# Mask buffers cut to the size in use in an attention and FFN kernel, and where the buffers behind them begin

## The chip, the cores and the metric

The kernel runs on one core of one Trainium2 chip. The metric is the device time of one execution in microseconds. In the profile, PE is TensorE's matmul, PEld its weight load, DVE is VectorE, ACT is ScalarE, POOL is GpSimd, and SP is the engine whose queue issues nearly all DMAs.

## The reference

A banded (sliding window) attention is followed by a feed-forward network (FFN) with two weight matrices. The batch is 8, with 8 heads, 576 tokens and a head dimension of 64, so the FFN sees 4608 tokens of 512 values; its inner width is 2048. Everything is float32.

```
scores = scale * np.matmul(q, k.transpose(0, 1, 3, 2))
mask = (rel >= 0) & (rel < window)          # rel = query - key position, window = 64
scores = np.where(mask, scores, -1000000000.0)
attn = softmax(scores)
x = (attn @ v) as [4608 tokens, 512]
h = x @ w_in                                # 512 -> 2048
g = np.where(h >= 1, h, np.where(h <= -1, 0.0, (h + 1) ** 2 / 4))
out = g @ w_out                             # 2048 -> 512
```

## The kernel before

The tokens are cut into nine FFN tiles of 512, and each of them into four attention steps of 128 tokens. An attention step loads qt, kt and two vt tiles, makes the scores on PE (L418), adds a mask and scales on DVE (L435), takes the row maximum (L439), the exponentials on ACT (L446) and the division (L458), transposes the probabilities into ptd (L464 on DVE; L479 on PE for the first steps) and multiplies them with vt (L493). The result is one block of x.

The FFN works in float32r, a float32 type that TensorE takes in one pass, with each number split into a high and a low part: x into xh and xl, each weight into the two halves of a wts buffer, each gate into gh and gl. A product is made as high times high, high times low and low times high, so each matmul appears three times. In a matmul, lhsT is the stationary operand (loaded by PEld) and rhs the moving one (streamed by PE).

- L898 (`ffn_in`), for the first three tiles: stationary is a wts block of 128 columns, moving is xh or xl, 512 columns (256 where a tile is done in halves).
- L831 (`ffn_product`), for the other six tiles, which go in three pairs: each pair's first layer is computed from seven products of sums of blocks in place of eight. Stationary is a piece of the ring, which is loaded from DRAM into freed weights buffers; moving is one of six x operands, split into high and low. Two of the six lie in xs buffers (which share the memory of xh1 and xl1), the other four in freed wts buffers. In the profile's names these are `ps_h<-xs,wts` and `ps_h<-wts`.
- L950 (`ffn_out`), the second layer, for all tiles: stationary is a block of 128 columns of gh or gl, moving is a wts half of 512 columns.
- Between the layers, the gate runs through ACT (L911, L916, L928), DVE (L923) and POOL or DVE (L933). For the pairs, first-layer sums stand in h buffers (L846, in the memory of xh0 and xl0), and some are spilled to DRAM and loaded back.

The order on every engine is fixed when the program is built: a planner (`Plan`) places each step by a key and a cost table of constants, and nothing in it reads a buffer's address. Two masks concern the change. `nmsk` holds three mask variants for the steps that use 32-row queries and 96 keys; it is declared with three rows of 128 columns, of which 96 are loaded (L400) and read (L433). `mskr` is a rounded copy of `msk` for the first four steps, whose mask is added by a matmul (L412); it is declared with three variants, of which two are written (L404). `nm` and `den` (L424) hold the negated maxima and the sums, 2 x 4 numbers a step, two buffers each.

On-chip buffers are laid out in each partition in this order, one behind the other: constants (idt, msk, nmsk, idr, mskr, ptd), the x pool (xh0/h, xl0/h, xh1/xs, xl1/xs), loads (kt, qt, vt), attention (sm, nm, den), FFN (u, a, gh, gl, o), weights. Start addresses of the program before, in bytes:

| buffer | begins at | past a multiple of 256 | past a multiple of 512 |
|---|---|---|---|
| idt (first constant) | 2176 | 128 | 128 |
| nmsk | 4224 | 128 | 128 |
| ptd | 7808 | 128 | 128 |
| xh0 / h | 13952 | 128 | 128 |
| kt | 46720 | 128 | 128 |
| sm | 65152 | 128 | 128 |
| nm | 73344 | 128 | 128 |
| u | 73472 | 0 | 256 |
| a (first gate buffer) | 81664 | 0 | 256 |
| first weights buffer | 98048 | 0 | 256 |

All other buffers of a kind follow at multiples of 512 or, for kt (3072 bytes) and the like, of 1024.

Of the kernel before, what the change touches and what calls it, by code (L numbers as in the profile page):

```python
# [10 lines left out]
F32 = mybir.dt.float32  # L11
F32R = mybir.dt.float32r
# [8 lines left out]
P = 128  # L21
QB = 64
SB = 2 * QB
WIN = 128
WINDOW = 64
SQ = 32
NEAR = WINDOW + SQ
# [174 lines left out]
def banded_attention_then_ffn(ctx: ExitStack, tc: tile.TileContext, q, k, v, w, masks, out, dims):  # L202
    nc = tc.nc
    B, H, S, D = dims
    NT, DM = out.shape
    NP = H // 2
# [3 lines left out]
    scale = 1.0 / float(D) ** 0.5  # L210
    TMAX = max(TILES)

    const = ctx.enter_context(tc.tile_pool(name="const", bufs=1))
    xpool = ctx.enter_context(tc.tile_pool(name="xpool", bufs=1))
    ld = ctx.enter_context(tc.tile_pool(name="ld", bufs=2))
    att = ctx.enter_context(tc.tile_pool(name="att", bufs=4))
# [9 lines left out]
    def banks_of_heads(pool):  # L226
        return bank(pool).rearrange("p (a n) -> p a n", a=NP)
# [1 line left out]
    idt = const.tile([P, P], F32, name="idt")  # L229
    make_identity(nc, idt)  # L230
    msk = const.tile([P, 3, WIN], F32, name="msk")
    nmsk = const.tile([P, 3, WIN], F32, name="nmsk")
    idr = const.tile([P, P], F32R, name="idr")
    mskr = const.tile([P, 3, WIN], F32R, name="mskr")
    wpool = ctx.enter_context(tc.tile_pool(name="wpool", bufs=1))
    dram = ctx.enter_context(tc.tile_pool(name="dram", bufs=1, space=bass.MemoryType.DRAM))
    kept = [dram.tile([P, 7, 2, 2, P], F32, name=f"kept{n}") for n in range(NF // 2)]
# [3 lines left out]
    for n, at in ((P, QB), (QB, 0)):  # L241
# [4 lines left out]
            out=m, in_=m, compare_op=ALU.is_ge, fill=NEG, base=at - 1, pattern=[[1, WIN]], channel_multiplier=-1  # L246
        )
        nc.gpsimd.affine_select(
            out=m, in_=m, compare_op=ALU.is_ge, fill=NEG, base=WINDOW - at, pattern=[[-1, WIN]], channel_multiplier=1
# [129 lines left out]
    def variant(s):  # L379
        firsts = [(2 * s + i) % NB == 0 for i in range(2)]  # L380
        return 1 if firsts[0] else 2 if firsts[1] else 0

    def near(s):
        return s >= PE_STEPS
# [12 lines left out]
        nc.sync.dma_start(out=t, in_=v[b * QB:b * QB + WIN])  # L397

    def load_masks():
        nc.sync.dma_start(out=nmsk[:, :, :NEAR], in_=masks)  # L400

    def round_masks():
        nc.scalar.copy(idr, idt)
        nc.scalar.mul(mskr[:, :2], msk[:, :2], 1.0 / scale)  # L404

    def att_scores(s, masked, pool):
        qt, kt = qts.pop(s), kts.pop(s)
        banks = [banks_of_heads(pool) for _ in range(2)]
        if masked:
            m = mskr[:, variant(s), :].unsqueeze(1).broadcast_to([P, NP, WIN])  # L410
            for ps in banks:
                nc.tensor.matmul(ps.rearrange("p a n -> p (a n)"), lhsT=idr, rhs=m, start=True, stop=False)  # L412
        m, n = (SQ, NEAR) if near(s) else (QB, WIN)
        for p in range(NP):
            for i in range(SB // m):
                r = slice(i * m, (i + 1) * m)
                for h in range(2):
                    nc.tensor.matmul(  # L418
                        banks[h][r, p, :n], lhsT=qt[half[h], p, r], rhs=kt[half[h], p, i * m:i * m + n],
                        start=not masked, stop=not masked or p == NP - 1,  # L420
                    )
        sm = att.tile([P, 2 * NP * WIN], F32, name="sm", bufs=BUFS["sm"])[:, :2 * NP * n]
        sm = sm.rearrange("p (h a n) -> p h a n", h=2, n=n)
        nm, den = (att.tile([P, 2, NP], F32, name=n, bufs=2) for n in ("nm", "den"))  # L424
        for h in range(2):
            blk[s, h] = banks[h][:, :, :n], sm[:, h], nm[:, h], den[:, h]
        blk[s, BOTH] = None, sm, nm, den
# [171 lines left out]
    def add_step(t, i):  # L599
# [15 lines left out]
        if s == 0:  # L615
            last["r"] = add(lk, dict(ACT=480), lambda e: round_masks())
        if s == PE_STEPS - 2:
            last["m"] = add(lk + M_LATE, dict(SP=590), lambda e: load_masks(), lag=DMA_LAG)
# [6 lines left out]
        if before:  # L625
            sv, (needs_v, gives_v, split) = before.popitem()

            def do(e):
                att_scores(s, masked, ps)
                att_values(sv, "ps_h")  # L630

            xs = add(
                key, dict(PE=B_PE), do, needs + needs_v, takes=[ps, ps, "sm", "ps_h"],
                gives=[("qt", xq), ("kt", xk)] + gives_v,
            )
            split(xs, key, "ps_h")
        else:
            xs = add(
                key, dict(PE=S_PE[near(s)] + 500 * masked), lambda e: att_scores(s, masked, ps), needs,
                takes=[ps, ps, "sm"], gives=[("qt", xq), ("kt", xk)],  # L640
            )
# [599 lines left out]
```

## Time and profile before

| what | us |
|---|---|
| median of three runs | 888.4 (886.26 to 888.56) |
| profiled execution | 887.9 |
| its span, first to last instruction | 886.0 |
| PE busy in the span | 866.9 |
| DVE busy | 646.3 |
| ACT busy | 499.4 |
| POOL busy | 190.9 |

The span is the time from the first to the last instruction of the profiled execution; 1.9 us of that execution lie around it. PE's busy time adds up pipelined matmuls whose ends are modelled, so the duration of one matmul in a row (some 390 ns) is longer than the time until the next one starts. Where a text speaks of the step of a matmul, it means the time from one start to the next. In the chain's rows, the columns are start, length and what ran, both in us. In the timeline's rows they are start, length up to the end of the last matmul, and the group. In a row of groups, the two numbers behind the first bar are busy us and mean ns of one instruction, and behind the second bar stands the idle time before them.

### The profile page before, as it was taken

The numbers are of one execution on the slowest core, as the hardware profiler recorded it, in microseconds if no ns is written. First come the engines' busy times: TensorE is split into PE (matmuls) and PEld (weight loads), VectorE is DVE, ScalarE is ACT, GpSimd is POOL, SyncE is SP. The second block draws the span as 40 slices with busy tenths as digits, with TensorE's granted clock in tenths as the row PEclk, the third lists the DMA queues.
The fourth block names the chain that finished last, engine by engine and source line by source line (L and its number), as shares of the span: only waits on it lengthen the run. The fifth ranks groups of instructions, "written<-read, shape, count | busy, mean of one in ns | idle before, by whom it ended". The sixth has DMA issues, their size and how long they took to land.

```text
span 886.0 us, 17772 instructions
## 1 busy us (share of the span) xinstructions
PE 866.9 (98%) x6687; PEld 699.8 (79%) x6687; DVE 646.3 (73%) x1278; ACT 499.4 (56%) x1246; POOL 190.9 (22%) x202
## 2 busy tenths in 40 slices
PE   7899999999999999999999999999999999999998
PEld 5778887877777788877878788887887888888786
DVE  6999997888877776797888985587889633333443
ACT  6999965556464656545346864443548643333464
POOL 1000045554422352121113331111130011111000
PEclk8999999999999999999999999999999999999999
DMA  9992179445333313667666606676544045554221
GB/s 320 419 361 86 40 214 322 126 150 180 130 126 126 108 55 119 231 204 226 188 198 191 205 13 202 187 215 203 176 137 155 24 140 170 160 158 147 100 100 48
DMA packets 88372, 147.57 MB, mean 167 GB/s; under 512 B 7776, under 2 KB 36704, under 8 KB 88288
## 3 DMA queue, kind: packets, MB, share of 16 engines
q1 hardware_dynamic: 88000, 145.53, 50.9%
q8 instruction: 53, 0.87, 0.4%
q10 hardware_dynamic: 288, 0.92, 0.3%
q14 instruction: 31, 0.25, 0.1%
HBM read 112.86 MB, written 33.55 MB: 165 GB/s over the span
## 4 chain that ended last, share of the span: by engine, by line
PE 86%; DVE 6%; DMA 5%; ACT 2%; POOL 1%; issue 1%; ACTq 0%; DVEq 0%; POOLq 0%
PE acc L950 40%; PE ps_h L831 26%; PE ps_h L898 12%; PE ps_a L493 3%; PE ps_a L418 3%; DMA raw<-in_w 3%; DVE ptd L464 1%; DVE sm L458 1%; DMA kept<-u 1%; DVE a L923 1%; DMA out<-o 1%; ACT sm L446 1%; DMA kept<-o 1%; DVE gl L933 0%; DVE h L846 0%
## 5 line engine op out<-in xcount | busy, mean ns | idle before, releaser
L950 PE MATMUL acc<-wts,gh 128*128 128x512 f32 x1154 | 362.2, 395 | 2.1 <-ACT h L274 2.0
L950 PEld LDWEIGHTS acc<-wts,gh 128*128 128x128 f32 x1154 | 212.9, 188 | 51.5 <-ACT h L274 3.3
L950 PE MATMUL acc<-wts,gl 128*128 128x512 f32 x577 | 225.8, 391 | 1.4 <-DVE gl L933 0.8
L933 POOL TENSOR_TENSOR gl<-a,gh 128x512 fp32r<-128x512 f32 (+1 forms) x82 | 105.2, 1283 | 440.9 <-ACT gh L928 430.5
L831 PE MATMUL ps_h<-wts 128*128 128x512 f32 x720 | 179.1, 390 | 0.0
L831 PEld LDWEIGHTS ps_h<-wts 128*128 128x128 f32 x720 | 134.7, 188 | 28.7
L464 DVE STREAM_TRANSPOSE ptd<-sm 32x256 f32<-32x256 f32 x336 | 146.5, 436 | 6.3 <-PE ps_a L493 0.3
L846 DVE TENSOR_TENSOR h<-h,ps_h 128x512 f32<-128x512 f32 x120 | 82.2, 685 | 80.1 <-PE ps_h L831 79.0
L928 ACT CAST gh<-a 128x512 fp32r<-128x512 f32 (+1 forms) x149 | 89.5, 602 | 87.5 <-DVE a L923 79.4
L898 PE MATMUL ps_h<-xh,wts 128*128 128x512 f32 (+1 forms) x424 | 133.6, 382 | 4.6 <-DVE a L923 3.3
L950 PEld LDWEIGHTS acc<-wts,gl 128*128 128x128 f32 x577 | 108.4, 188 | 27.2 <-DVE gl L933 2.4
L911 ACT ACTIVATE a<-h 128x512 f32<-128x512 f32 x96 | 60.3, 631 | 101.2 <-DVE h L846 74.1
L923 DVE SCALAR_TENSOR_TENSOR a<-a,h 128x512 f32<-128x512 f32 x96 | 67.1, 700 | 65.5 <-ACT a L916 63.7
L446 ACT ACTIVATE sm<-sm,nm 128x96 f32<-128x96 f32 (+1 forms) x256 | 93.2, 366 | 19.0 <-DVE nm L439 19.0
L898 PEld LDWEIGHTS ps_h<-xh,wts 128*128 128x128 f32 x424 | 78.5, 191 | 21.5 <-DVE a L923 4.3
L916 ACT ACTIVATE a<-a 128x512 f32<-128x512 f32 (+1 forms) x136 | 83.8, 616 | 4.2
L898 PE MATMUL ps_h<-xl,wts 128*128 128x512 f32 (+1 forms) x212 | 80.0, 377 | 0.5 <-DVE xl L506 0.5
L831 PE MATMUL ps_h<-xs,wts 128*128 128x512 f32 x288 | 75.0, 395 | 0.0
L274 ACT COPY h<-ps_h 128x512 f32<-128x512 f32 x46 | 27.0, 587 | 74.4 <-PE ps_h L831 74.1
L831 PEld LDWEIGHTS ps_h<-xs,wts 128*128 128x128 f32 x288 | 53.7, 188 | 12.1
L911 ACT ACTIVATE a<-ps_h 128x512 f32<-128x512 f32 (+1 forms) x53 | 29.4, 554 | 42.1 <-PE ps_h L898 39.5
L933 DVE TENSOR_TENSOR gl<-a,gh 128x512 fp32r<-128x512 f32 (+1 forms) x67 | 44.7, 668 | 7.7 <-ACT gh L928 7.3
(106 smaller groups left out, 837.7 us busy)
## 6 DMA issues: line engine op xcount, KB each, us to landing
wts<-kept SPq DMA_DIRECT2D x168, 256.0 KB, 3.0
vt<-in_v SPq DMA_DIRECT2D x72, 256.0 KB, 3.6
kt<-in_k SPq DMA_DIRECT2D x35, 384.0 KB, 4.3
raw<-in_w SPq DMA_DIRECT2D x12, 1023.8 KB, 11.3
qt<-in_q SPq DMA_DIRECT2D x36, 256.0 KB, 3.1
spill<-h SPq DMA_DIRECT2D x18, 512.0 KB, 3.0
h<-spill SPq DMA_DIRECT2D x18, 512.0 KB, 3.7
out<-o SPq DMA_DIRECT2D x27, 256.0 KB, 2.5
```

Of the source, the lines that this page charges most:

```text
L274: nc.scalar.copy(dst, src)
L446: nc.scalar.activation(sm[:, p, :], (ps if masked else sm)[:, p, :], AF.Exp, bias=nm[:, p:p + 1], scale=scale if masked else 1.0, accum_ou ...
L464: nc.vector.transpose(dst[:, :, r], src[:, :, c * SQ:(c + 1) * SQ])
L831: nc.tensor.matmul(ps, lhsT=r[:, part, cp], rhs=x_op(k, xp)[:, cp], start=j in (0, 1, 3, 4) and i == 0 and cp == 0, stop=j in (1, 2, 5, 6) ...
L846: nc.vector.tensor_tensor(out=h[:, to], in0=h[:, of], in1=prods[u, n, b], op=ALU.add)
L898: nc.tensor.matmul(ps, lhsT=wts[f, 0][:, part, c * P:(c + 1) * P], rhs=x[:, c, r], start=(c == 0 and j == 0), stop=(c == NP - 1 and j == 2),)
L911: nc.scalar.activation(gs[t, f, r.start][0], phs[t, f, r.start], AF.Relu, bias=0.5, scale=0.5)
L916: nc.scalar.activation(a, a, AF.Square)
L923: nc.vector.scalar_tensor_tensor(out=a, in0=a, scalar=1.0, in1=ps, op0=ALU.min, op1=ALU.max)
L928: nc.scalar.copy(g[1], g[0])
L933: engine[eng].tensor_tensor(out=g[2], in0=g[0], in1=g[1].bitcast(F32), op=ALU.subtract)
L950: nc.tensor.matmul(acc[t, i][:, n], lhsT=g[:, sub], rhs=wts[f, 1][:, part, n], start=(q == 0 and j == 0), stop=(q == NF - 1 and j == 2 and ...
```

## The change

Three declarations shrink or grow, and three uses are adapted to them. `nmsk` gets rows of 96 columns in place of 128, so the transfer that fills it writes one contiguous run in a partition. `mskr` gets two variants in place of three. `nm` and `den` are taken from buffers of twice the size, of which the first half is used. No instruction is added or removed.

```
-    nmsk = const.tile([P, 3, WIN], F32, name="nmsk")
+    nmsk = const.tile([P, 3, NEAR], F32, name="nmsk")
     idr = const.tile([P, P], F32R, name="idr")
-    mskr = const.tile([P, 3, WIN], F32R, name="mskr")
+    mskr = const.tile([P, 2, WIN], F32R, name="mskr")
...
     def load_masks():
-        nc.sync.dma_start(out=nmsk[:, :, :NEAR], in_=masks)
+        nc.sync.dma_start(out=nmsk, in_=masks)
 
     def round_masks():
         nc.scalar.copy(idr, idt)
-        nc.scalar.mul(mskr[:, :2], msk[:, :2], 1.0 / scale)
+        nc.scalar.mul(mskr, msk[:, :2], 1.0 / scale)
...
-        nm, den = (att.tile([P, 2, NP], F32, name=n, bufs=2) for n in ("nm", "den"))
+        nm, den = (att.tile([P, 4, NP], F32, name=n, bufs=2)[:, :2] for n in ("nm", "den"))
```

(WIN is 128, NEAR is 96, NP is 4, P is 128 partitions; a float32 has 4 bytes.)

## The prediction

> **What bounds the kernel now.** I read the page first (busy time, slices, the chain that ended last), then the PE groups by shape, then the chain and the PE timeline in short windows, and last the DMA issues.
>
> ```profile
> span 886.0 us, 17772 instructions
> PE 866.9 (98%) x6687; PEld 699.8 (79%) x6687; DVE 646.3 (73%) x1278; ACT 499.4 (56%) x1246; POOL 190.9 (22%) x202
> PEclk8999999999999999999999999999999999999999
> PE 86%; DVE 6%; DMA 5%; ACT 2%; POOL 1%; issue 1%; ACTq 0%; DVEq 0%; POOLq 0%
> ```
>
> PE is busy for 98% of the span at its full granted clock, and it holds 86% of the chain. So the pace of the matmuls sets the time, and a change that touches no instruction can still count, if it alters how fast PE takes one matmul after another. The groups that matter are the 128x512 ones; their operands lie in buffers whose addresses the change moves.
>
> ```profile
> L950 PE MATMUL acc<-wts,gh 128*128 128x512 f32 x1150 | 361.5, 395 | 2.1 <-ACT h L274 2.0
> L950 PE MATMUL acc<-wts,gl 128*128 128x512 f32 x575 | 225.3, 392 | 1.4 <-DVE gl L933 0.8 <-POOL gl L933 0.6
> L831 PE MATMUL ps_h<-wts 128*128 128x512 f32 x720 | 179.1, 390 | 0.0
> L898 PE MATMUL ps_h<-xh,wts 128*128 128x512 f32 x344 | 116.9, 401 | 2.3 <-DVE a L923 2.3
> L831 PE MATMUL ps_h<-xs,wts 128*128 128x512 f32 x288 | 75.0, 395 | 0.0
> L898 PE MATMUL ps_h<-xl,wts 128*128 128x512 f32 x172 | 68.2, 396 | 0.0
> ```
>
> The durations (390 to 401 ns) overlap one another, so they don't give the pace. The step from one start to the next does. Line 831 offers a comparison within one line: the same stationary operand (a piece of the ring, in a weights buffer), the same shape and type, and a moving operand that lies sometimes in a weights buffer (720 matmuls) and sometimes in an xs buffer (288). On the timeline two such runs of six, one of each kind, stand next to L950; the chain gives their lengths.
>
> ```profile
> 517.25 1.52 PE L831 MATMUL ps_h<-wts 128*128 128x512 f32 x6
> 532.21 1.55 PE L831 MATMUL ps_h<-xs,wts 128*128 128x512 f32 x6
> ```
>
> ```profile
> 517.42 1.36 PE ps_h L831 x6
> 518.78 13.60 PE acc L950 x60
> 532.38 1.39 PE ps_h L831 x6
> 533.77 1.37 PE acc L950 x6
> ```
>
> Six with the moving operand in a weights buffer take 1.36 us, sixty of L950 (moving operand again in a weights buffer) take 13.60 us: 226.7 ns a step both times. Six with it in an xs buffer take 1.39 us, 231.7 ns a step, and the six behind them 1.37. Now line 898, whose moving operands xh and xl lie in the x buffers:
>
> ```profile
> 302.33 2.94 PE acc L950 x12
> 306.35 2.98 PE ps_h L898 x12
> 309.33 2.77 PE acc L950 x12
> 312.10 5.60 PE ps_h L898 x24
> ```
>
> Twenty-four of L898 take 5.60 us, 233.3 ns a step. The rows at 302.33 and 306.35 start behind attention matmuls: there L950 as well is slow for some steps (2.94 us for twelve, of which about 0.11 is one long step at the start), and L898 takes 0.04 more.
>
> **Where the buffers lie.** In the program before, the constants begin at byte 2176 of a partition. Adding up the buffers in the order of allocation, the x, h, xs, kt, qt, vt, sm and ptd buffers all begin 128 bytes past a multiple of 256 (the first x buffer at 13952 = 54 x 256 + 128). Then nm and den, four times 32 bytes, bring u, the gates (a, gh, gl), o and the weights to a multiple of 256 (the first gate buffer at 81664 = 319 x 256). So the slow moving operands are those of the 128-byte offset, the fast ones those of a multiple of 256.
>
> **The change part by part.** nmsk loses 3 x 32 x 4 = 384 bytes and mskr 512. Everything from ptd to sm moves down by 896 = 3.5 x 256 bytes, so the x and attention buffers get a multiple of 256. nm and den grow by 32 bytes each, four buffers, 128 in all: everything behind them moves by 768 = 3 x 256. Gates and weights thus keep their multiple of 256; what is new for them is that they come from 256 past a multiple of 512 to a multiple of 512 (81664 - 768 = 80896 = 158 x 512). No instruction is added, removed or moved: the planner's costs are constants, and no wait comes or goes.
>
> *Term 1, the x matmuls.* From the start times in the trace (all steps between two 128x512 matmuls that are under 260 ns): xs 231.9 ns on 280 steps, xh and xl 232.5 on 476, L831 from weights buffers 227.1 on 700, L950 228.3 on 1625. Against the even pace of 226.7 the excess is 5.2 x 288 = 1.5 us for xs and 5.8 x (344 + 172) = 3.0 us for xh and xl: 4.5 us.
>
> *Term 2, the runs behind them.* Where L950 or L831-from-weights follows an x run without a break, the first four steps are 231.8, 232.0, 230.6 and 227.9 ns on the mean of 62 such places, 15.5 ns more than four even ones: 62 x 15.5 = 1.0 us. This goes with the cause.
>
> *Term 3, what stays.* A run behind attention matmuls starts unevenly whatever it reads: in L950, with its multiple of 256, by some 30 ns a run over its first nine steps (mean of 29 such runs). 17 x runs start so (13 of L898, 4 of L831), and will go on to: 17 x 30 = 0.5 us of term 1 stay. PE sum: 4.5 + 1.0 - 0.5 = 5.0 us.
>
> *What doesn't arrive.* From 132 to 228 us the chain is mostly off PE:
>
> ```profile
> 132.75 4.57 DMA kept<-o
> 137.32 6.04 DMA out<-o
> 178.82 4.83 DMA kept<-u
> ```
>
> 139 of the 756 counted x steps lie there, 18%, or 0.9 us of the sum; I take two thirds of it as lost to these waits, 0.6. From 50 to 132 us DVE is nearly as full as PE:
>
> ```profile
> 50.00:132.00 82.00, 82.00 (x568) 66.17 (x567) 80.23 (x146) 72.15 (x145) 8.51 (x12) 1.00 0.48 166
> ```
>
> 145 steps, 1.0 us; I take a third as lost to DVE, 0.3. That leaves 5.0 - 0.9 = 4.1 us.
>
> *Attention matmuls.* vt and ptd reach a multiple of 256 too; kt and qt are read at steps of 128 bytes, so as many reads come into line as go out of it.
>
> ```profile
> L493 PE MATMUL ps_a<-ptd,vt 128*64 128x64 f32 x992 | 35.7, 225 | 0.9 <-DVE ptd L276 0.9
> L898 PE MATMUL ps_h<-xh,wts 128*128 128x256 f32 x80 | 16.8, 298 | 2.3 <-DVE xh L276 1.4 <-DVE a L923 0.9
> L950 PE MATMUL acc<-wts,gh 128*128 128x256 f32 x4 | 0.8, 282 | 0.0
> 232.27 1.08 PE ps_a L493 x32
> 236.31 0.93 PE ps_a L418 x55
> ```
>
> L493 takes 1.08 us for a block of 32. If each of its some 36 blocks (1,152 matmuls with those into other banks) lost 16 x 5 ns, that would be 36 x 0.08 = 2.9 us; the lower bound is nothing, and below it I see no reason for a loss. I take nothing: the nearest rows of short moving operands, the 128x256 ones, step from start to start at 119.6 ns in L898 with its offset of 128 (mean of 64 steps) and at 114 to 120 in L950's four without. The x matmuls of that width are costed at nothing for the same reason.
>
> *ACT and DVE.* ACT takes as long from an h buffer (128 past) as from a gate buffer:
>
> ```profile
> L911 ACT ACTIVATE a<-h 128x512 f32<-128x512 f32 x96 | 60.3, 631 | 101.2 <-DVE h L846 74.1 <-DVE gl L933 21.2 <-POOL gl L933 2.1
> L916 ACT ACTIVATE a<-a 128x512 f32<-128x512 f32 x126 | 79.7, 632 | 4.0
> ```
>
> 631 against 632 ns: I cost these engines at nothing.
>
> *Transfers.* The masks come in as one run of 1152 bytes in a partition in place of three of 384. That one transfer is issued at 36.1 us and takes 11.1 to landing, and its first reader starts at 113.4, 66 us after it lands, so whatever it saves is hidden.
>
> ```profile
> L435 DVE SCALAR_TENSOR_TENSOR sm<-ps_a,nmsk x58: 505/548/559, 113.4 to 650.4; 128x384 f32<-128x384 f32 x58
> L400 SPq DMA_DIRECT2D nmsk<-in_masks x1: 648/648/648, 36.1 to 36.1; - x1
> ```
>
> ```profile
> nmsk<-in_masks SPq DMA_DIRECT2D x1, 144.0 KB, 11.1
> qt<-in_q SPq DMA_DIRECT2D x36, 256.0 KB, 3.1
> wts<-kept SPq DMA_DIRECT2D x168, 256.0 KB, 3.0
> ```
>
> q, with the offset, and the ring's loads, without it, are of one size and land in 3.1 and 3.0 us; a tenth of a microsecond on loads that PE hardly waits for is worth 0, and if a few waits shorten by it, under 0.5 us.
>
> The profiled execution took 887.9 us (886.0 of span and 1.9 around it), 0.5 below the median of the three runs, 888.4. 887.9 - 4.1 = 883.8 us.
>
> **The rivals.** *A, only the 16-byte line counts.* The offset could be a bystander, and the x buffers slow for another reason that the change leaves (their region of the memory, or who last wrote them). Then nothing moves: 887.9 us. For it: no buffer changes its offset within the trace, so place and offset can't be separated here. Against it: on line 831 the pace changes within one run of the same work, and the x copies that lie in weights buffers, written by the same engines, go at 226.7. The Trainium skill stands with this rival: "SBUF — State Buffer", section "Specifications (TRN2)", gives the memory lines of 16 bytes and a penalty only for crossing into a new one, by which every start here, 128 past included, is in line already and the change is worth nothing. The 231.7 and 226.7 ns above disagree with that reading, and no run here shows yet which of the two is right.
>
> *B, relative place.* If moving and stationary operand have to agree beyond 256 bytes (weights and gates now agree to 512 among themselves; after the change x stands 256 off them), x gains about half: 887.9 - 2 = 885.9.
>
> *C, more than forecast.* Attention's 2.9 us and the 0.9 that I held back both arrive: 887.9 - 7.9 = 880.0.
>
> *D, slower.* Gates and weights get starts at multiples of 512, which no buffer of the FFN has now. If such a start costs what 128 past costs now, 5.2 ns, the 1150 + 575 + 720 matmuls that move weights lose 2445 x 5.2 = 12.7 us, and the time is 887.9 - 4.1 + 12.7 = 896.5. It decides from 4.1 us / 2445 = 1.7 ns a matmul on. For it: nothing in the profile excludes it. Against it: each moving operand is 2048 bytes long and passes multiples of 512 wherever it starts, and L950's gates are read at starts 512 bytes apart, all at one pace.
>
> **How the numbers follow.** Forecast 0.60, A 0.18, B 0.07, C 0.07, D 0.08. A measurement of this kernel tells about 0.3%, 2.7 us, from no change: faster means under 885.7. The forecast, C and a part of B, less the part of the forecast that loses more on the way, make 0.66 faster; A and the rest 0.26 the same; D 0.08 slower. The range goes from C's side to A: 880.4 to 887.9. That leaves out D, half of C and the upper spread of A, nearly 2 in 10.
>
> **What would show it.** Right: L831 from xs takes 1.36 us for six, L898 takes 5.45 for twenty-four, L950 behind L898 2.73 for twelve, while ACT and DVE keep their means. Wrong: these keep their steps (A), come to about 229 ns on the mean (B), or L950's long runs leave 226.7 (D upward). If the steps fall to 226.7 and the time falls by less than 3 us, it is the share that I let arrive that failed.

## The result and the profile after

| | before | after |
|---|---|---|
| median, us (6 runs each) | 887.73 (886.26 to 888.56) | 882.15 (880.94 to 883.11) |
| profiled execution | 887.9 | 880.95 |
| its span | 886.0 | 879.1 |

The ratio is 0.9936, with a 95% interval of 0.9923 to 0.995: faster by 5.6 us. A second measurement of the same kernel, told below, gave 0.9963 (0.995 to 0.9976), 3.9 us.

The page of the changed kernel has the same instructions as before, and PE is as full as it was:

```profile
span 879.1 us, 17772 instructions
PE 858.8 (98%) x6687; PEld 697.3 (79%) x6687; DVE 644.0 (73%) x1278; ACT 499.1 (57%) x1246; POOL 195.0 (22%) x202
PE 87%; DVE 7%; DMA 3%; ACT 2%; issue 1%; POOL 0%; ACTq 0%; SPq 0%; DVEq 0%; POOLq 0%
DMA packets 88116, 147.57 MB, mean 168 GB/s; under 512 B 7392, under 2 KB 36448, under 8 KB 88032
```

PE's busy time moved most, 866.9 to 858.8. The small packets are fewer by 384, 7776 to 7392: the masks' three runs of 384 bytes on each of 128 partitions have become one run of 1152.

The chain of the changed kernel at the places that the prediction quoted (start, length, what ran):

```profile
511.78 1.36 PE ps_h L831 x6
513.14 13.60 PE acc L950 x60
526.74 1.36 PE ps_h L831 x6
528.10 1.36 PE acc L950 x6
```

```profile
298.28 2.96 PE acc L950 x12
302.32 2.95 PE ps_h L898 x12
305.27 2.72 PE acc L950 x12
307.99 5.44 PE ps_h L898 x24
```

Six matmuls from xs now take 1.36 us as six from a weights buffer do (1.39 before), twenty-four of L898 take 5.44 (5.60), and the twelve of L950 behind L898 take 2.72 (2.77). Behind attention matmuls a run starts as unevenly as ever (2.96). Sixty of L950 take 13.60 as before, so their move to multiples of 512 did nothing.

Over the whole trace, a step being the time from one start to the next (all steps between two 128x512 matmuls under 260 ns):

| moving operand | before, ns | after, ns |
|---|---|---|
| L831 from xs | 231.9 | 227.2 |
| L898 (xh, xl) | 232.5 | 227.8 |
| L831 from weights buffers | 227.1 | 227.0 |
| L950 (weights) | 228.3 | 227.7 |

The sum of what these steps (some 3,090) take over the even 226.7 ns, called the excess below, fell from 7.05 to 2.56 us: 4.5 us.

### The profile page after: what moved, and what is told of

The parts are those of the page before. It is cut to its first block, busy times and chain, and to the rows that moved or that the text cites. A ratio compares the mean times of both kernels' runs of the same rounds, so it can differ in the third digit from the quotient of the medians.

```text
span 879.1 us, 17772 instructions
## 1 busy us (share of the span) xinstructions
PE 858.8 (98%) x6687; PEld 697.3 (79%) x6687; DVE 644.0 (73%) x1278; ACT 499.1 (57%) x1246; POOL 195.0 (22%) x202
## 2 busy tenths in 40 slices
DMA packets 88116, 147.57 MB, mean 168 GB/s; under 512 B 7392, under 2 KB 36448, under 8 KB 88032
## 4 chain that ended last, share of the span: by engine, by line
PE 87%; DVE 7%; DMA 3%; ACT 2%; issue 1%; POOL 0%; ACTq 0%; SPq 0%; DVEq 0%; POOLq 0%
PE acc L950 41%; PE ps_h L831 26%; PE ps_h L898 12%; PE ps_a L418 3%; PE ps_a L493 3%; DVE ptd L464 2%; DMA out<-o 1%; DVE a L923 1%; DVE sm L458 1%; DMA vt<-in_v 1%; DMA raw<-in_w 1%; ACT sm L446 1%; DMA kept<-u 0%; PE ps_h L493 0%; DVE h L846 0%
## 5 line engine op out<-in xcount | busy, mean ns | idle before, releaser
L950 PE MATMUL acc<-wts,gh 128*128 128x512 f32 x1154 | 360.8, 394 | 2.0 <-ACT h L274 2.0
L950 PEld LDWEIGHTS acc<-wts,gh 128*128 128x128 f32 x1154 | 212.7, 188 | 49.7 <-ACT h L274 3.3
L950 PE MATMUL acc<-wts,gl 128*128 128x512 f32 x577 | 225.3, 391 | 1.2 <-DVE gl L933 0.8
L831 PE MATMUL ps_h<-wts 128*128 128x512 f32 x720 | 179.0, 390 | 0.0
L831 PEld LDWEIGHTS ps_h<-wts 128*128 128x128 f32 x720 | 134.7, 188 | 28.6
L898 PE MATMUL ps_h<-xh,wts 128*128 128x512 f32 (+1 forms) x424 | 130.2, 374 | 5.3 <-DVE a L923 3.6
L950 PEld LDWEIGHTS acc<-wts,gl 128*128 128x128 f32 x577 | 108.3, 188 | 26.0 <-DVE gl L933 2.1
L446 ACT ACTIVATE sm<-sm,nm 128x96 f32<-128x96 f32 (+1 forms) x256 | 93.2, 367 | 18.6 <-DVE nm L439 18.6
L898 PEld LDWEIGHTS ps_h<-xh,wts 128*128 128x128 f32 x424 | 77.4, 188 | 20.9 <-DVE a L923 4.6
L898 PE MATMUL ps_h<-xl,wts 128*128 128x512 f32 (+1 forms) x212 | 78.5, 370 | 0.6 <-DVE xl L506 0.6
L831 PE MATMUL ps_h<-xs,wts 128*128 128x512 f32 x288 | 73.6, 391 | 0.0
L831 PEld LDWEIGHTS ps_h<-xs,wts 128*128 128x128 f32 x288 | 53.8, 188 | 11.4
```

The source lines that it names most:

```text
L446: nc.scalar.activation(sm[:, p, :], (ps if masked else sm)[:, p, :], AF.Exp, bias=nm[:, p:p + 1], scale=scale if masked else 1.0, accum_ou ...
L831: nc.tensor.matmul(ps, lhsT=r[:, part, cp], rhs=x_op(k, xp)[:, cp], start=j in (0, 1, 3, 4) and i == 0 and cp == 0, stop=j in (1, 2, 5, 6) ...
L898: nc.tensor.matmul(ps, lhsT=wts[f, 0][:, part, c * P:(c + 1) * P], rhs=x[:, c, r], start=(c == 0 and j == 0), stop=(c == NP - 1 and j == 2),)
L950: nc.tensor.matmul(acc[t, i][:, n], lhsT=g[:, sub], rhs=wts[f, 1][:, part, n], start=(q == 0 and j == 0), stop=(q == NF - 1 and j == 2 and ...
```

## The experiments

Each kernel is the changed one with pads, small buffers that are set to zero once and never read, so that chosen buffers begin elsewhere. All compute the whole reference. The pads shift the lines by up to three (L834 is L831). A place is given in bytes past a multiple of 256. Each ratio is to the kernel before, measured beside the run (886.9 to 887.0 us here). At the end stands a table of all runs.

**x and the loads back to 128 (x_off).** `pad_c` has 128 bytes and stands ahead of ptd; `pad_a` has 384 and stands ahead of sm.

```
+    pad_c = const.tile([P, 32], F32, name="pad_c")
+    nc.gpsimd.memset(pad_c, 0.0)
+    nc.gpsimd.memset(att.tile([P, 96], F32, name="pad_a", bufs=1), 0.0)
     ptq = const.tile([P, BUFS["ptd"], NP, SB], F32, name="ptd")
```

> The changed kernel with a pad of 128 bytes ahead of ptd and one of 384 behind the value loads: ptd, x, h, xs, kt, qt and vt begin 128 bytes past a multiple of 256 again, while the masks stay short and sm, gates and weights stay at a multiple of 256 (gates and weights of 512). Theory (the start of the moving operand within 256 bytes sets the step of a 128x512 matmul): the x matmuls go back to 231.9 to 232.5 ns a step and the runs behind them to about 231, which is 4.4 us: 882.2 + 4.4 = 886.6. Rival (the gain comes from the shorter masks, or from gates and weights going to a multiple of 512): the x steps stay at 227.2 to 227.8 and the time at 882.

The chain of this run:

```profile
517.30 13.60 PE acc L953 x60
530.90 1.39 PE ps_h L834 x6
532.29 1.37 PE acc L953 x6
```

Measured: 887.02 us, ratio 0.9994 (0.9983 to 1.0005). With the short masks still in place, the steps and the time of before are back. So the gain comes from where x, and ptd and the loads with it, begin, and not from the shorter masks or from the shift of gates and weights alone.

**sm, gates and weights to 128, x left (w_off).** The pad: 128 bytes ahead of sm.

```
+    nc.gpsimd.memset(att.tile([P, 32], F32, name="pad_a", bufs=1), 0.0)
```

> The changed kernel with a pad of 128 bytes ahead of sm: sm, gates and weights begin 128 bytes past a multiple of 256, x and the loads stay at one. Theory (absolute start of the moving operand): L950 and L831 from weights buffers, which move weights, go from 227.0 to 227.7 ns to about 232, L898 and L831 from xs stay at 227; 2445 x 4.7 ns = 11.5 us, so about 893.7. Rival one (moving and stationary operand must agree): L950 and L831 from weights buffers, where both are shifted alike, stay at 227, and L898 and L831 from xs, where only the stationary one is shifted, go to about 232; 804 x 4.8 = 3.9 us, 886. Rival two (the stationary operand's start counts as well): all groups slow down, 15 us or more.

The chain of this run, at both places:

```profile
516.53 13.60 PE acc L951 x60
530.13 1.39 PE ps_h L832 x6
531.53 1.38 PE acc L951 x6
```

```profile
307.11 2.77 PE acc L951 x12
309.88 5.60 PE ps_h L899 x24
```

Here L950 moves weights that begin 128 past, and its sixty still take 13.60 us. The longer steps are those of L831 from xs (1.39) and L898 (5.60), although x itself begins at a multiple of 256. Time 886.91, ratio 1.0001 (0.999 to 1.0012). My theory, the absolute start of the moving operand, falls; it asked for 893.7. Rival one stands: where the steps are long, the moving operand (x) and the stationary one (a weights buffer) begin at different places within 256 bytes; where they are short, at the same.

**Gates and weights 256 past a multiple of 512 (w_256).** As w_off, with a pad of 256 bytes.

> The changed kernel with a pad of 256 bytes ahead of sm: gates and weights begin 256 bytes past a multiple of 512, as before the change, and x stays where the change put it. Theory (256 bytes decide, 512 don't): steps and time as in the changed kernel, 882.2 within 1. Rival (part of the gain comes from gates and weights at multiples of 512): the steps of L950 go up by some tenths of a ns, and the time by up to 1.2 us, which is what the x steps don't account for, 883.4.

Measured: 882.56, ratio 0.9952 (0.9936 to 0.9967), every mean step within 0.1 ns of the changed kernel's. In the changed kernel x stands 256 bytes off the weights within 512, here they agree to 512: no difference. A shift of 256 bytes between the two operands costs nothing.

**Only kt, qt and vt to 128 (att_off).** A pad of 128 bytes behind the x buffers and one of 128 behind the value loads; its reference is w_256.

> The changed kernel with a pad of 128 bytes behind the x buffers and one of 128 behind the value loads: kt, qt and vt alone begin 128 bytes past a multiple of 256 (gates and weights stand 256 past a multiple of 512, as in the run with the pad of 256). Theory (short moving operands and loads don't feel the offset): 882.2 within 1, L493 at 1.08 us for a block of 32. Rival (the part of the gain that the x steps don't account for is the attention's): 883.4, with L493 at more than in the changed kernel or with loads of q, k and v that land later.

The chain of this run:

```profile
302.20 1.08 PE ps_a L494 x32
306.23 2.72 PE acc L953 x12
308.95 5.44 PE ps_h L901 x24
```

Measured: 882.68, ratio 0.9952 (0.9935 to 0.9969), against 882.56 of w_256. L493 takes 1.08 us for 32 (here L494), as in the kernel before. Its two operands disagree here (vt at 128, ptd at 0), so the matmuls of 64 columns don't feel a difference of 128. The scores (L418) tell less, since qt and kt moved together. The loads landed alike within 0.1 us, with the offset and without: q after 3.2 and 3.1 us, k after 4.1 and 4.2, v after 3.6 both times.

**Everything to 128 (all_off).** Pads of 128 bytes ahead of ptd and 512 behind the value loads.

> The changed kernel with a pad of 128 bytes ahead of ptd and one of 512 behind the value loads: everything from ptd on, x, loads, sm, gates and weights, begins 128 bytes past a multiple of 256. New theory (the moving and the stationary operand of the float32r matmuls have to begin at the same place within 256 bytes; the place itself doesn't count): all steps stay at 227 to 228 ns and the time at 882.5. The first theory (the moving operand has to begin at a multiple of 256) is left only if the x steps go to 232; then all the others should, too, which the run with shifted weights has not shown. Rival (the x groups want both operands at a multiple of 256, L950 doesn't): x steps at 232 and 887.

The chain of this run:

```profile
515.42 13.60 PE acc L953 x60
529.02 1.36 PE ps_h L834 x6
530.38 0.68 PE acc L953 x3
```

Measured: 883.36, ratio 0.9952 (0.9938 to 0.9967). No buffer of the FFN begins at a multiple of 256, and all steps are as short as in the changed kernel. So it is agreement that counts, not the multiple.

**x at 64, 192 and 32 (x_64, x_192, x_32).** As x_off, with the two pads chosen so that sm, gates and weights stay at 0.

> The changed kernel with a pad of 64 bytes ahead of ptd and one of 448 behind the value loads: x and the loads 64 past a multiple of 256, sm, gates and weights at one. If any difference within 256 bytes costs alike, the x steps go to 232 and the time to 887. If the cost grows with the distance (128 is the farthest), the x steps come to about 229.5 and the time to 884.8. If a shift by some part of a line helps, the x steps fall below 226.7.

> The changed kernel with a pad of 192 bytes ahead of ptd and one of 320 behind the value loads: x and the loads 192 past a multiple of 256 (64 short of the next), sm, gates and weights at one. Cost alike for any difference: x steps at 232, 887. Cost by distance: as with 64, 229.5 and 884.8. Cost by direction (the moving operand ahead of the stationary one or behind it): another value than with 64.

> The changed kernel with a pad of 32 bytes ahead of ptd and one of 480 behind the value loads: x and the loads 32 past a multiple of 256, sm, gates and weights at one. Cost alike for any difference: 232 ns and 887. Cost by distance: about 228 ns and 883.6. Units of 64 bytes (a start within the first 64 counts as none): 227.3 ns and 882.5.

The chain of the run with 32:

```profile
519.11 13.60 PE acc L953 x60
532.71 1.40 PE ps_h L834 x6
534.11 1.39 PE acc L953 x6
```

Line 898 (here L901), with 64 and then with 192:

```profile
310.22 5.52 PE ps_h L901 x24
```

```profile
312.20 5.60 PE ps_h L901 x24
```

Measured: 887.81 with 64, 888.55 with 192, 888.42 with 32 (ratios 1.0008, 1.0019 and 1.0018, each within 0.0012). Each of these differences costs the gain, and 32 bytes cost no less than 128; a cost that grows with the distance is out. None of the means falls below 226.7 ns. With 64 the x steps themselves are a little better (L898 229.9), but the runs behind them worse (L831 from weights buffers 228.6), which comes to the same. 64 and 192 are equally far from agreement, and L898 takes 229.9 ns a step with one and 233.2 with the other: the cost is not alike in both directions, and why is open.

**The changed kernel again (after_again).**

> The changed kernel itself, unaltered, on the chip of the two runs beside it. The steps account for 4.4 us, the first measurement gave 5.6 (ratio 0.9936, 0.9923 to 0.995). If the 1.2 between them is scatter, the ratio comes to 0.995, as with the runs that kept x and weights in agreement; if it belongs to this very layout, it stays near 0.9936.

Measured: 883.01, ratio 0.9963 (0.995 to 0.9976). The first measurement's 5.6 us held some scatter; all agreeing kernels measured later gained 3.6 to 4.3 on the median.

**sm, u and gates to 128, x and weights left (g_off).** A pad of 128 ahead of sm, and one of 128 behind the gates:

```
         g.append(gate_tile("gl", F32R, r))
+        if (t, f) == (0, 0) and r.start == 0:
+            nc.gpsimd.memset(ffn.tile([P, 32], F32, name="pad_f", bufs=1), 0.0)
```

> The changed kernel with a pad of 128 bytes ahead of sm and one of 128 behind the gates: sm, u and the gates begin 128 bytes past a multiple of 256; x, o and the weights at one. New theory (moving and stationary operand have to agree within 256 bytes): L950, whose stationary operand is a gate and whose moving one is a weight, goes from 227.7 to about 232.5 ns, x steps stay at 227 to 228; 1725 x 5.2 = 9 us, so 891. Rival (the x buffers' own start within 256 bytes against the weights' is special, gates play no part): nothing changes, 882.5.

The chain of this run:

```profile
515.80 1.37 PE ps_h L832 x6
517.17 13.95 PE acc L953 x60
531.12 1.37 PE ps_h L832 x6
532.49 1.40 PE acc L953 x6
```

Measured: 890.75, ratio 1.0048 (1.0033 to 1.0063). Now L950 has the long steps, 13.95 us for sixty, 232.5 ns a step, which no layout so far had made of it; L831 keeps 1.37. L898's mean rose to 229.0, since its neighbours have the long steps now. Nothing special about x, then.

**Weights and o to 128, x and gates left (w_alone).** The second pad of g_off alone.

> The changed kernel with a pad of 128 bytes behind the gates: o and the weights begin 128 bytes past a multiple of 256; x and the gates at one. New theory: L950, L898 and L831 from xs all go to about 232, and L831 from weights buffers, with both operands in weights buffers, stays at 227; (1725 + 804) x 5.2 = 13 us, so 895.5. Rival (only x against weights counts): L898 and L831 from xs go to 232, L950 stays; 887.

The chain of this run:

```profile
521.08 13.95 PE acc L952 x60
535.02 1.38 PE ps_h L831 x6
536.40 1.39 PE acc L952 x6
```

```profile
309.83 2.79 PE acc L952 x12
312.62 5.60 PE ps_h L898 x24
```

Measured: 895.19, ratio 1.0097 (1.0083 to 1.011). L950 and L898 both have the long steps, as expected. L831 from weights buffers agrees in itself; its mean rose to 229.4 because nearly all its neighbours have them.

| kernel | x | gates | weights | xs | L898 | L831 weights | L950 | excess, us | median, us |
|---|---|---|---|---|---|---|---|---|---|
| before | 128 | 0 | 0 | 231.9 | 232.5 | 227.1 | 228.3 | 7.05 | 887.73 |
| after | 0 | 0 | 0 | 227.2 | 227.8 | 227.0 | 227.7 | 2.56 | 882.15 |
| after_again | 0 | 0 | 0 | 227.2 | 227.8 | 227.1 | 227.7 | 2.59 | 883.01 |
| w_256 | 0 | 0 | 0 | 227.2 | 227.8 | 227.0 | 227.7 | 2.56 | 882.56 |
| att_off | 0 | 0 | 0 | 227.2 | 227.8 | 227.1 | 227.7 | 2.60 | 882.68 |
| all_off | 128 | 128 | 128 | 227.2 | 227.8 | 227.0 | 227.7 | 2.59 | 883.36 |
| x_off | 128 | 0 | 0 | 231.9 | 232.5 | 227.1 | 228.2 | 6.99 | 887.02 |
| w_off | 0 | 128 | 128 | 231.9 | 232.5 | 227.1 | 228.2 | 7.04 | 886.91 |
| x_64 | 64 | 0 | 0 | 231.5 | 229.9 | 228.6 | 228.7 | 7.56 | 887.81 |
| x_192 | 192 | 0 | 0 | 233.2 | 233.2 | 227.4 | 228.5 | 8.22 | 888.55 |
| x_32 | 32 | 0 | 0 | 233.6 | 233.5 | 227.4 | 228.5 | 8.60 | 888.42 |
| g_off | 0 | 128 | 0 | 228.1 | 229.0 | 227.7 | 232.6 | 11.87 | 890.75 |
| w_alone | 0 | 0 | 128 | 231.4 | 232.4 | 229.4 | 232.5 | 15.40 | 895.19 |

The four step columns are means in ns, the excess is the sum of all counted steps over 226.7 ns. The first two medians come from the first measurement, the others from the experiments. From the group at 2.6 to the group at 7.0 the excess grows by 4.4 us and the time by 4.5 (882.56 in w_256 to 887.02 in x_off, taken side by side); to w_alone by 12.8 and 12.2 (from 883.01, side by side).

## Why the prediction was right, point by point

**The sign and the place** were right: the x matmuls of L831 and L898 lost their extra 5 ns a step, and the runs behind them lost theirs.

**Where the buffers lie.** The prediction put the long steps down to the moving operand's 128-byte offset and the short ones to its multiple of 256. That was true of the kernel before, but as a cause it was wrong. all_off has every operand at the offset, and its x steps are short; w_off has x at a multiple, and they are long. What counts is that the moving and the stationary operand begin at the same place within 256 bytes. The prediction named relative place only as rival B, and there in a form that w_256 refutes (agreement beyond 256). In the trace of before, the two readings could not be told apart, since all stationary operands lay at a multiple of 256; a kernel that shifts the other operand was needed.

**Terms 1 to 3.** The prediction had 5.0 us on PE; the counted steps gave 4.5. Term 2 came out in full: the four steps behind an x run are now 226.5, 226.9, 227.2 and 226.6 on the mean of 65 places (15.5 ns too many before, 0.4 now). Term 1 was too large for two reasons. It charged all 804 x matmuls, while the counted x steps had 4.2 us of excess, not 4.5. And it held back too little: 0.66 us of that stayed, not 0.5, since the runs behind attention matmuls and in the early tiles stay uneven.

**What doesn't arrive** was the step that failed, as a size. I took 0.9 us off for the stretch on DMAs and for DVE; the four sets taken side by side (the first, and those of w_256 with att_off, of all_off and of after_again) gain 5.6, 4.3, 4.0 and 3.3 us on the mean, together about 4.3. They scatter by more than 2 us, but their middle lies near the 4.5 that the steps lose, not near the 3.6 that would be left after holding back 0.9. The traces show in part where. The table takes each stage between the same matmuls in every execution, named by their times in the kernel before; "apart" are before, x_off and w_off, where x and weights differ by 128, "agreeing" are after, after_again, w_256, att_off and all_off.

| stage, us | excess apart | excess agreeing | time apart | time agreeing |
|---|---|---|---|---|
| 50 to 132 | 1.1 | 0.6 | 82.0 to 82.1 | 81.5 to 81.6 |
| 132 to 228 | 1.2 | 0.3 to 0.4 | 94.8 to 96.1 | 93.2 to 95.0 |
| 228 to 345 | 1.7 | 0.5 | 117.0 to 117.1 | 116.0 to 117.1 |
| 345 to the last | 2.9 to 3.0 | 1.0 to 1.1 | 537.0 to 537.1 | 534.6 to 535.3 |

From 50 to 132 us the steps lose 0.5 us and the time the same, though DVE is nearly full: holding back 0.3 there was wrong. (Of the prediction's 145 steps 133 lie in that window, the others before it.) From 132 to 228 us kernels with equal steps differ by 1.3 and 1.9 us, more than the 0.8 in question, so these traces don't tell what the waits there swallow. From 228 to 345 us, where nothing was held back, three of the five agreeing kernels gain 1.0 us or more, but after itself gains nothing in its profiled execution. Of the DMAs on the changed kernel's chain between 132 and 228 us these are the longest:

```profile
135.98 5.93 DMA out<-o
175.36 4.16 DMA kept<-u
```

The two errors, a PE sum too high by 0.5 us and 0.9 held back, nearly cancelled: 4.1 us were forecast, 3.9 and 5.6 measured, and 4.3 to 4.5 is what the sets together and the steps give. That the forecast came so close is luck in part.

**At nothing** I had costed the attention matmuls (att_off bears it out), the 128x256 matmuls (119.7 ns a step before, 119.8 after), the transfers, and ACT:

```profile
L911 ACT ACTIVATE a<-h 128x512 f32<-128x512 f32 x96 | 60.3, 631 | 99.2 <-DVE h L846 73.4 <-DVE gl L933 19.7 <-POOL gl L933 2.4
L916 ACT ACTIVATE a<-a 128x512 f32<-128x512 f32 x126 | 79.7, 633 | 3.9
```

631 ns, as before, though h begins elsewhere within 256 bytes.

**The rivals.** A is out: the change took the long steps away, and pads alone bring them back. Nor are all starts at multiples of 16 alike: 32 bytes of difference cost 5.1 us (x_32 at 888.42, all_off beside it at 883.36). C's larger gain was not there. D's premise is out, since starts at a multiple of 512 cost nothing. A loss of that kind exists, though, where gates and weights are shifted against each other: w_alone and g_off lose 12.2 and 7.7 us against the changed kernel beside them.

Why the two starts must agree is not shown; no run here looks inside. On the trace, agreeing streams settle to 226 and 227 ns within about ten steps of a run's start, and the disagreeing ones go on in a repeating pattern (225 to 232 ns in x_64, 230 to 235 in x_32). "TensorE: Matmul & The Clock Gate" of the Trainium skill, section "Part 2: What happens when you issue a matmul", says that the moving operand and the weight load have independent read ports and that loading weights doesn't take read bandwidth from the running matmul. By that, w_off and all_off would be alike. They differ by 4.7 ns a step on L831 from xs, so for these float32r matmuls the measurement decides against it.

## What to carry to other kernels

Where a kernel streams 512-wide float32r matmuls with a fresh weight load for each, let the stationary and the moving operand begin at the same place within 256 bytes; here a mismatch cost about 5 ns of 227, 2%, on each matmul that had it (3 to 4 at a difference of 64). A few odd bytes in a small buffer can shift one pool against another, so look at start addresses, and compare steps from start to start instead of durations. An offset seen on one operand alone proves nothing about that operand: shift the other one before you name the cause.

## What the runs showed of the hardware that was not expected

The step of a 128x512 float32r matmul depends on the difference of its two operands' starts modulo 256 bytes: 227 to 228 ns on the mean at 0 (with both at 0 or both at 128, and 226.7 in long runs), 231 to 234 at 32, 128 and 192, 230 to 231.5 at 64. The effect doesn't grow with the difference, and it spills into the four or so matmuls behind the mismatched run (62 x 15.5 ns, about 1 us, in the kernel before). Plain float32 matmuls of 64 columns showed nothing of it at a difference of 128, nor did 256-wide float32r ones (119.7 ns a step against 119.8). With x at 32 and 192 these 256-wide steps were shorter, 117 ns; no run here asks why.
